# The float64 weights' decode: the sign carried by ScalarE's leaky relu, and the magnitudes written in bfloat16

## The chip, the cores and the metric

The kernel runs on one core of one Trainium2 chip. The metric is device microseconds of that core for one execution. The core has five engines that run their own instruction streams in order and wait for each other by semaphores: TensorE (PE in the profile, its weight loads as PEld), VectorE (DVE), ScalarE (ACT), GpSimd (POOL) and SyncE (SP), which here issues the DMAs.

## The reference

Three blocks follow each other. The inputs are q, k, v of 4 batches, 8 heads, 576 positions, 64 channels.

```
bias   = relu((log1p|i-j| / log1p(max(i,1))) * w1 + b1) @ w2     # per head, 576 x 576
attn   = softmax(q @ k.T / 8 + bias)
x      = attn @ v                                                # 2304 x 512
h      = max(x @ moe_w1, x @ moe_w2, x @ moe_w3)                 # 512 -> 768
x      = h @ moe_w_out                                           # 768 -> 512
h      = x @ moe2_w_in                                           # 512 -> 2048
g      = h where h >= 1, 0 where h <= -1, else (h + 1)^2 / 4
out    = g @ moe2_w_out                                          # 2048 -> 512
```

The six weight matrices of the last two blocks reach the kernel as 64-bit floats: `_layout` hands them over as 64-bit words, and the kernel itself has to turn each into a 32-bit float before it can use it. That turning is the place of the change.

## The kernel before

Every product with a weight is done in three float16 passes: a weight is split into a high float16 part and a low float16 rest (`split`, L155 to L163: ScalarE writes the high part at L158, VectorE the rest at L159), the other operand likewise, and TensorE multiplies high by high, high by low and low by high.

A weight piece is a 128 x 512 block. It goes through these steps:

- `raw_load` (L423): SyncE issues a DMA that brings the block as 64-bit words into a raw buffer.
- `decode` (L430 to L439): four operations on the two 32-bit halves of each word, below.
- `sum_scale` (L448 to L457) or `pair_scale` (L516 to L527): TensorE multiplies the piece's magnitudes with a matrix of ones (L454, L522), so that each column's sum of magnitudes stands in PSUM; VectorE takes the largest (L456, L525) and makes a power of two of it (L137, L138, L142). The magnitudes are read in bfloat16, by `high(y)`.
- `split` by that power of two (L158, L159).

`decode` works on the high word of a 64-bit float (sign, 11 exponent bits, 20 mantissa bits) and on the low word (32 mantissa bits). L435 reads the high word as a 32-bit float and multiplies it by a power of two on ScalarE, which lowers the exponent and keeps the sign; the result is z. L436 makes the top three bits of the low word on ScalarE; that is y. L437 on VectorE shifts z left by three and puts y's bits beside it: y is now the magnitude as a 32-bit float, the shift having pushed the sign out. L438 on VectorE takes the sign bit of z and puts it on y: z is now the weight. `high(y)` is the upper 16 bits of every 32-bit word of y, a bfloat16 with a step of two.

There are 56 pieces. `conv_moe` (18 of them, three per call, names `ws`, `ab`, `aw` for the raw buffers) decodes in place and puts y where the split weight will stand; `conv_wo` (6, raw buffer `ws`); `late_pieces` (32, two at a time), whose raw buffers are `ws` and `v`, whose z is a tile `sp` from a pool of four that the softmax shares, and whose y is the place where the weight will live (`ab`, `masks`, `rw`, `xtab`, `ws`, `k`). The next raw load into a buffer can start only when both L435 and L436 have read it.

Around this, attention runs in 144 slots. A slot's scores come from TensorE (L662), VectorE adds the bias and takes the row's extreme (L674), ScalarE exponentiates (L676), ScalarE and GpSimd split the result in two float16 parts (L692, L693, L694), a DMA transposes them (L696; in half of the first block's slots TensorE transposes instead, L681 to L688), and TensorE multiplies by v (L716). The first MLP (L771 to L783, then L793 to L799) and the bias of the next blocks are mixed in between, then the second MLP follows: L1002 to L1044 for the first block, L1080 to L1131 for the rest. The program fixes each engine's order of instructions when it is built: a scheduler lays the instructions out by priority and by a timeline that it plans, so a change in one helper moves others on every engine.

Of the kernel before, what the change touches and what calls it, by code (L numbers as in the profile page):

```python
# [8 lines left out]
BF16 = mybir.dt.bfloat16  # L9
F32 = mybir.dt.float32  # L10
U32 = mybir.dt.uint32
I64 = mybir.dt.int64
AF = mybir.ActivationFunctionType
ALU = mybir.AluOpType
# [6 lines left out]
def kernel(ctx: ExitStack, tc: tile.TileContext, qt, kt, vr, small, mw1, mw2, mw3, mwo, win, wo2, out):  # L21
# [7 lines left out]
    V, A, G, T, SP = nc.vector, nc.scalar, nc.gpsimd, nc.tensor, nc.sync  # L29
# [135 lines left out]
    if True:  # L165
# [73 lines left out]
        for j in range(5):  # L239
            i0, n = BLK[j][0], BLK[j][1]  # L240
# [16 lines left out]
        for g in range(4):  # L257
            p = slice(32 * g, 32 * g + 32)
# [171 lines left out]
        def decode(r, z, y):  # L430

            w = r.bitcast(U32).rearrange("p (n two) -> p n two", two=2)
            if z is None:
                z = w[:, :, 1]
            A.activation(z.bitcast(F32), w[:, :, 1].bitcast(F32), AF.Copy, scale=2.0 ** -112)  # L435
            A.activation(y, w[:, :, 0], AF.Copy, scale=2.0 ** -29 * (1 - 2.0 ** -20), bias=-0.5)  # L436
            V.scalar_tensor_tensor(y, z, 3, y, ALU.logical_shift_left, ALU.bitwise_or)  # L437
            V.scalar_tensor_tensor(z, z, 0x80000000, y, ALU.bitwise_and, ALU.bitwise_or)  # L438
            return z.bitcast(F32)  # L439

        def high(y):

            return y.bitcast(BF16).rearrange("p (n two) -> p n two", two=2)[:, :, 1]

        def by_k(t):
            return t.rearrange("p (k f) -> p k f", k=KK)
# [1 line left out]
        def sum_scale(s, ys):  # L448

            pn = mlp_ps()  # L450
            for i, y in enumerate(ys):
                yb = high(y)
                for k in range(KK):
                    T.matmul(pn[:, P * i:P * i + P], ones, yb[:, P * k:P * k + P], start=(k == 0), stop=(k == KK - 1))  # L454
            t = st([P, 1], F32, "tcol")
            V.tensor_reduce(t, pn[:, :P * len(ys)], AX.X, ALU.max)  # L456
            pow2_inverse(s, t, 14)  # L457

        def conv_moe(ft):

            zs, ys = [], []
            for i in range(3):
                ys.append(wm[:, ft, i].rearrange("p s k c -> p (s k c)").bitcast(U32))
                zs.append(decode(moe_raw[3 * ft + i], None, ys[-1]))
            s = c_sn[:, ft:ft + 1]
            sum_scale(s, ys)
            for i in range(3):
                split(wm[:, ft, i, 0], wm[:, ft, i, 1], by_k(zs[i]), s, WENG[i])
            if ft == 0:
                moe_load(4)  # L470
            if ft == 3:
                moe_load(5)

        def conv_wo():

            zs = []
            for ft in range(NF1):
                raw_load(mwo[P * ft:P * ft + P, :], raws[:, ft % 2])
                y = rt_[:, ft % 2]
                zs.append(decode(raws[:, ft % 2], zt[:, ft] if ft < 5 else rt_[:, 0], y))  # L480
                sum_scale(c_sm[:, ft:ft + 1], [y])
                yield
            t = newcol(NF1)
            V.tensor_tensor(t, c_sn, c_sm, ALU.mult)
            V.tensor_reduce(c_kap, t, AX.X, ALU.min)
            inv2(t, c_sn)
            V.tensor_scalar(c_sm, t, c_kap, None, ALU.mult)
            for ft in range(NF1):
                split(wo16[:, ft, 0], wo16[:, ft, 1], zs[ft], c_sm[:, ft:ft + 1], "v")
                yield  # L490
# [25 lines left out]
        def pair_scale(s, ys, k):  # L516

            pn = mlp_ps()
            for i, y in enumerate(ys):
                yb = high(y)  # L520
                for kk in range(KK):
                    T.matmul(pn[:, P * i:P * i + P], ones, yb[:, P * kk:P * kk + P], start=(kk == 0), stop=(kk == KK - 1))  # L522
            n = s.shape[1]
            t = st([P, 2], F32, "tcol2")[:, :n]
            V.tensor_reduce(t, pn[:, :2 * P].rearrange("p (n c) -> p n c", n=n), AX.X, ALU.max)  # L525
            floor2(t, t)
            inv2(s, t, k)  # L527

        def late_pieces():
# [19 lines left out]
            for y in range(len(spec) // 2):  # L549
                load(2 * y + 2)  # L550
                dst = [late_home(2 * y + i) for i in range(2)]
                zs = [decode(loaded[2 * y + i], st([P, S], F32, "sp")[:, :512].bitcast(U32), dst[i].bitcast(U32)) for i in range(2)]
                load(2 * y + 3)
                q = y // 2
                s = c_sq2[:, q:q + 1] if y % 2 else c_sp[:, 2 * q:2 * q + 2]
                pair_scale(s, [d.bitcast(U32) for d in dst], 12 if y % 2 else 14)
                for i in range(2):
                    split(dst[i][:, 0:512], dst[i][:, 512:1024], zs[i], s[:, 0:1] if y % 2 else s[:, i:i + 1], PENG[y % 2])
                yield
                yield  # L560
# [580 lines left out]
        for x in range(len(work) + GL):  # L1141
            if x < len(work):
                y, sub, ft = work[x]
# [17 lines left out]
            if x >= GL:  # L1161
                y, sub, ft = work[x - GL]
# [48 lines left out]
```

## Time and profile before

| what | value |
|---|---|
| median of 3 runs | 1063.61 us (1061.68 to 1063.82) |
| span of the profiled execution, first to last instruction | 1056.6 us |
| time around the span: median less span | 7.0 us |
| PE busy | 948.6 us, 90% |
| DVE busy | 753.9 us, 71% |
| ACT busy | 572.4 us, 54% |
| POOL busy | 489.5 us, 46% |
| the chain that ended last, by engine | PE 55%, DVE 19%, DMA 8%, ACT 6%, POOL 5% |

The profile is of one execution that is not among the three timed ones, so its own whole time is known as its span, and the 7.0 us are the difference to the median of the runs. Busy time is an average over stages with different limits; the stages used here are cut by time: 38 to 125 us (the first slots, and all of `conv_moe`), 125 to 240 (`conv_wo`), 240 to 470, 470 to 590, 590 to 690 us (most of `late_pieces`), and from 690 us on, where no weight is decoded.

### The profile page before, as it was taken

The numbers are of one execution on the slowest core, as the hardware profiler recorded it, in microseconds if no ns is written. First come the engines' busy times: TensorE is split into PE (matmuls) and PEld (weight loads), VectorE is DVE, ScalarE is ACT, GpSimd is POOL, SyncE is SP. The second block draws the span as 40 slices with busy tenths as digits, with TensorE's granted clock in tenths as the row PEclk, the third lists the DMA queues.
The fourth block names the chain that finished last, engine by engine and source line by source line (L and its number), as shares of the span: only waits on it lengthen the run. The fifth ranks groups of instructions, "written<-read, shape, count | busy, mean of one in ns | idle before, by whom it ended". The sixth has DMA issues, their size and how long they took to land.

```text
span 1056.6 us, 26035 instructions
## 1 busy us (share of the span) xinstructions
PE 948.6 (90%) x10298; PEld 772.4 (73%) x10298; DVE 753.9 (71%) x1686; ACT 572.4 (54%) x1146; POOL 489.5 (46%) x705
## 2 busy tenths in 40 slices
PE   6787879799999989999899779989999999999993
PEld 5555768687788878777678667634588888888882
DVE  8989977887546677566475498698787586676662
ACT  4487665675665545775666466543344444444441
POOL 1032335577667754655456121887035344444340
PEclk7586789899999989999899899999999999999997
DMA  9796757599999888999997843010020010000000
GB/s 293 209 273 176 207 153 150 146 224 205 229 231 208 183 177 163 216 223 213 205 240 170 176 165 115 21 40 1 1 81 21 1 42 21 1 22 21 1 21 20
DMA packets 229437, 139.10 MB, mean 132 GB/s; under 512 B 177988, under 2 KB 208196, under 8 KB 228804
## 3 DMA queue, kind: packets, MB, share of 16 engines
q1 hardware_dynamic: 229316, 137.45, 54.9%
q8 instruction: 80, 1.31, 0.5%
q14 instruction: 41, 0.34, 0.1%
HBM read 79.68 MB, written 15.27 MB: 90 GB/s over the span
## 4 chain that ended last, share of the span: by engine, by line
PE 55%; DVE 19%; DMA 8%; ACT 6%; POOL 5%; issue 4%; SPq 1%; DVEq 0%; POOLq 0%; ACTq 0%
PE pm L1080 13%; PE pm L771 13%; PE s L1119 11%; PE s L662 6%; PE pav L716 3%; PE pm L793 3%; DVE sp L674 3%; DMA ws<-in_moe_w_out_dram 2%; PE s L1028 2%; PE pm L375 2%; DMA v<-in_moe_w_in_dram 1%; DVE aw L159 1%; DMA xT<-px 1%; ACT sp L676 1%; DVE phl L1020 1%
## 5 line engine op out<-in xcount | busy, mean ns | idle before, releaser
L771 PE MATMUL pm<-xT,aw 128*128 128x256 f16 (+1 forms) x2160 | 243.6, 266 | 17.0 <-DVE pt L688 4.4
L771 PEld LDWEIGHTS <-aw 128*128 128x128 f16 x2160 | 190.8, 100 | 55.2 <-issue 28.2
L676 ACT ACTIVATE sp<-sp,mx 128x576 f32<-128x576 f32 x144 | 110.5, 768 | 91.6 <-DVE mx L674 91.4
L694 POOL TENSOR_TENSOR phl<-sp,phl 128x512 f16<-128x512 f32 x128 | 154.4, 1206 | 0.1
L662 PE MATMUL s<-k,qz 64*128 64x288 f32 (+1 forms) x576 | 138.5, 470 | 12.2 <-DVE mx L674 11.4
L693 POOL TENSOR_TENSOR phl<-sp,phl 128x64 f16<-128x64 f32 x128 | 47.8, 373 | 211.9 <-ACT phl L692 151.8
L1097 ACT ACTIVATE sp<-pm,vec 128x256 f32<-128x256 f32 x112 | 61.3, 556 | 93.9 <-PE pm L1080 93.8
L674 DVE CUSTOM_DVE_ANT_0 sp<-s,ab 128x576 f32<-128x576 f32 x128 | 93.2, 749 | 18.8 <-PE s L662 10.3
L662 PEld LDWEIGHTS s<-k,qz 64*128 64x128 f32 (+1 forms) x576 | 75.7, 205 | 37.4 <-DVE mx L674 15.7
L1080 PEld LDWEIGHTS <-ab 128*128 128x128 f16 x840 | 82.1, 98 | 10.3
L793 PE MATMUL pm<-hh,wo 128*128 128x256 f16 x648 | 79.0, 276 | 11.5 <-ACT hh L782 7.4
L716 PEld LDWEIGHTS <-pt 128*128 128x128 f16 x1792 | 73.9, 99 | 15.6 <-issue 6.2
L692 ACT ACTIVATE phl<-sp 128x576 f16<-128x576 f32 x128 | 84.2, 672 | 1.0
L783 POOL TENSOR_TENSOR hh<-hm,hh 128x256 f16<-128x256 f32 (+1 forms) x60 | 41.7, 696 | 88.6 <-ACT hh L782 87.2
L1101 POOL TENSOR_TENSOR hh<-hh 128x128 f32<-128x128 f32 x56 | 32.7, 584 | 107.5 <-DVE hh L1099 101.2
L1098 DVE SCALAR_TENSOR_TENSOR hh<-pm,vec,sp 128x256 f32<-128x256 f32 x112 | 52.7, 478 | 35.0 <-ACT sp L1097 34.7
L793 PEld LDWEIGHTS <-wo 128*128 128x128 f16 x648 | 62.5, 99 | 20.3 <-issue 11.8
L716 PE MATMUL pav<-v,pt 128*128 128x64 f16 x1568 | 71.0, 195 | 2.6 <-ACT pt L685 1.5
L778 DVE SCALAR_TENSOR_TENSOR hm<-pm,hm 128x256 f32<-128x256 f32 (+1 forms) x120 | 46.9, 391 | 31.6 <-PE pm L771 15.8
L1119 PEld LDWEIGHTS <-xT 128*128 128x128 f16 x588 | 57.4, 98 | 7.8 <-ACT xT L1106 1.2
L1119 PEld LDWEIGHTS <-wo 128*128 128x128 f16 x588 | 57.5, 98 | 6.7
L1102 POOL TENSOR_TENSOR hh<-hh 128x128 f32<-128x128 f32 x56 | 25.8, 460 | 68.8 <-DVE hh L1099 64.1
(281 smaller groups left out, 1979.3 us busy)
## 6 DMA issues: line engine op xcount, KB each, us to landing
k<-in_k_dram SPq DMA_DIRECT2D x64, 288.0 KB, 4.3
v<-v_d SPq DMA_DIRECT2D x24, 640.0 KB, 5.1
ws<-in_moe_w_out_dram SPq DMA_DIRECT2D x15, 512.0 KB, 5.7
ws<-in_moe_w_in_dram SPq DMA_DIRECT2D x11, 512.0 KB, 4.8
x_d<-hl SPq DMA_DIRECT2D x36, 128.0 KB, 2.4
qz<-in_q_dram SPq DMA_DIRECT2D x16, 256.0 KB, 5.1
ab<-in_moe_w_dram SPq DMA_DIRECT2D x8, 512.0 KB, 8.7
qz<-x_d SPq DMA_DIRECT2D x4, 1024.0 KB, 4.8
```

Of the source, the lines that this page charges most:

```text
L662: T.matmul(sbox[i + r][:, c, :288], q[p, s if u.j == SJ else s // 2], k[p, 288 * c:288 * c + 288], start=True, stop=True)
L674: V.tensor_tensor_reduce(halves(sn), sbox.pop(i)[:, :, :288], halves(bias_sb[u.j][:, h]), -0.125, 3e38, ALU.add, ALU.min, mx)
L676: A.activation(pf, sn, AF.Exp, scale=-1.0, bias=mx, accum_out=u.sums[:, h:h + 1])
L692: A.activation(hl[:, :S], pf, AF.Copy)
L694: G.tensor_tensor(hl[:, S + 64:], pf[:, :512], hl[:, :512], ALU.subtract)
L716: T.matmul(u.pav[:, 64 * h:64 * h + 64], pt[:, c], v[:, sl, 64 * (h % 4):64 * (h % 4) + 64], **kw)
L771: T.matmul(o, wm[:, ft, i, wp, kk], x_rhs(key, xp, kk) if n == 256 else x_rhs(key, xp, kk)[:, c], start=(x == 0), stop=(x == 11))
L793: T.matmul(pm, wo16[:, ft, wp, P * d:P * d + P], hh[:, ft, hp], start=(ft == 0 and y == 0), stop=(ft == NF1 - 1 and y == 2))
L1080: T.matmul(pm, w[:, wp, kk], x2t[ORDER[y]][:, kk, xp, 256 * sub:256 * sub + 256], start=(x == 0), stop=(x == 11))
L1097: A.activation(r, pm, AF.Relu, scale=c_ch[:, f], bias=c_half)
L1098: V.scalar_tensor_tensor(t, pm, c_c[:, f], r, ALU.mult, ALU.max)
L1119: T.matmul(m[x], gl[:, gp, i], w[:, wp], start=(start and z == 0 and x % 2 == 0), stop=(stop and z == 2 and (x % 2 == 1 or x == 6)))
```

## The change

In `decode`, L435 turns from a copy with a scale into a leaky relu, in which positive and negative inputs get different powers of two. For a positive high word x the result is x times 2^-112, as before. For a negative one it is |x| times 2^-80: a positive number whose exponent is larger by 32. After the shift by three that difference sits in the sign bit, so that L437 alone yields the signed weight, in z. The second VectorE operation is gone. L438 is now a ScalarE operation that writes the weight's magnitude as bfloat16 into the first half of y's memory, and `high(y)` reads 512 bfloat16 values there, one beside the other. Per piece the kernel has three ScalarE operations and one VectorE operation where it had two and two; line numbers are the same before and after.

```diff
-            A.activation(z.bitcast(F32), w[:, :, 1].bitcast(F32), AF.Copy, scale=2.0 ** -112)
+            A.activation(z.bitcast(F32), w[:, :, 1].bitcast(F32), AF.Prelu, scale=-(2.0 ** -80), alpha=-(2.0 ** -32))
             A.activation(y, w[:, :, 0], AF.Copy, scale=2.0 ** -29 * (1 - 2.0 ** -20), bias=-0.5)
-            V.scalar_tensor_tensor(y, z, 3, y, ALU.logical_shift_left, ALU.bitwise_or)
-            V.scalar_tensor_tensor(z, z, 0x80000000, y, ALU.bitwise_and, ALU.bitwise_or)
+            V.scalar_tensor_tensor(z, z, 3, y, ALU.logical_shift_left, ALU.bitwise_or)
+            A.activation(high(y), z.bitcast(F32), AF.Abs)
             return z.bitcast(F32)
 
         def high(y):
 
-            return y.bitcast(BF16).rearrange("p (n two) -> p n two", two=2)[:, :, 1]
+            return y.bitcast(BF16)[:, 0:512]
```

The order of instructions moves with it. The first place is VectorE at the end of the first bias, where the first six pieces (`ws`, `ab`, `aw`) are put together between the first rows of the softmax (L674, named ISA here). A piece of the difference, - before, + after:

```order
-L437 SCALAR_TENSOR_TENSOR aw<-ws,aw 128x512 x2
-L437 SCALAR_TENSOR_TENSOR aw<-ab,aw 128x512
+L437 SCALAR_TENSOR_TENSOR ws<-ws,aw 128x512 x2
+L437 SCALAR_TENSOR_TENSOR ab<-ab,aw 128x512
 L437 SCALAR_TENSOR_TENSOR aw<-aw 128x512 x3
 L233 TENSOR_SCALAR btmp<-ident,tcol 128x128
 L674 ISA sp,mx<-s,ab 128x576
 L674 ISA mx 128x1
-L438 SCALAR_TENSOR_TENSOR ws<-ws,aw 128x512
 L288 TENSOR_SCALAR xtab<-xtab,vec 128x576
-L438 SCALAR_TENSOR_TENSOR ws<-ws,aw 128x512
-L438 SCALAR_TENSOR_TENSOR ab<-ab,aw 128x512
```

L437 now writes where the high word stood instead of y, and L438 no longer stands between the softmax's rows. The second place is ScalarE at the same time, from the last L435 of the first twelve pieces on:

```order
 L435 ACTIVATE aw<-aw 128x512 x3
 L435 ACTIVATE ab<-ab 128x512 x3
-L676 ACTIVATE sp,sums<-sp,mx 128x576
-L692 ACTIVATE phl<-sp 128x576
-L676 ACTIVATE sp,sums<-sp,mx 128x576 x2
+L438 ACTIVATE aw<-ws 128x512 x2
+L438 ACTIVATE aw<-ab 128x512
+L438 ACTIVATE aw<-aw 128x512 x3
```

All six L438 now stand ahead of the first exponential, L676. The third place is ScalarE in `late_pieces`, around 600 us. Before:

```order
L436 ACTIVATE ab<-v 128x512
L435 ACTIVATE sp<-v 128x512
L436 ACTIVATE ab<-ws 128x512
L776 ACTIVATE hm<-pm 128x256
L435 ACTIVATE sp<-ws 128x512
L782 ACTIVATE hh<-hm 128x256
```

The same place after the change:

```order
L436 ACTIVATE ab<-v 128x512
L438 ACTIVATE ab<-sp 128x512
L435 ACTIVATE sp<-v 128x512
L782 ACTIVATE hh<-hm 128x256
L776 ACTIVATE hm<-pm 128x256
L435 ACTIVATE sp<-ws 128x512
```

L438, which waits for VectorE's L437 of its piece, now stands ahead of an L435, and L436 of the piece in `ws` comes later than it did. SyncE issues the same DMAs, some of them in another order. ScalarE's order holds two table loads, at L219 and L249, before and after.

## Rows read from the trace of the kernel before

**Rows 1.** Busy us per stage: PE, PEld, DVE, ACT, POOL; clock, DMA
```profile
38.00:125.00 87.00, 68.61 (x512) 49.71 (x512) 78.38 (x169) 55.95 (x107) 24.27 (x30) 0.67 0.70 193
125.00:240.00 115.00, 101.44 (x1505) 84.18 (x1504) 94.65 (x225) 74.14 (x172) 63.34 (x82) 0.91 0.79 178
240.00:470.00 230.00, 220.75 (x2982) 186.19 (x2981) 145.50 (x355) 138.97 (x332) 143.86 (x196) 0.99 0.97 202
470.00:590.00 120.00, 104.25 (x1362) 84.67 (x1356) 69.22 (x160) 76.02 (x167) 63.84 (x88) 0.96 0.95 203
590.00:690.00 100.00, 87.81 (x735) 69.55 (x736) 78.06 (x217) 57.96 (x117) 37.29 (x37) 0.98 0.37 115
```

**Rows 2.** The same stages, VectorE's L438 alone: busy us (instructions)
```profile
38.00:125.00 87.00, 14.16 (x18) 0.67 0.70 193
125.00:240.00 115.00, 4.09 (x6) 0.91 0.79 178
240.00:470.00 230.00, 2.58 (x4) 0.99 0.97 202
470.00:590.00 120.00, 9.97 (x11) 0.96 0.95 203
590.00:690.00 100.00, 11.61 (x17) 0.98 0.37 115
690.00:1057.00 367.00, 0.00 (x0) 0.98 0.06 21
```

**Rows 3.** Chain that ended last, 38 to 125 us: start, us, what
```profile
44.08 0.60 DVE ws L438
...
50.45 0.02 ACT sp L676
...
75.83 3.30 ACT aw L436 x6
79.14 0.55 ACT ws L435
...
114.81 0.13 DVE ab L438
```

**Rows 4.** PE's waits, 38 to 125 us: total, times, longest
```profile
PE s L662 <- DVE mx L674: 9.4, 6, 3.1
...
PE pm L235 <- DVE btmp L233: 2.4, 2, 1.7
```

**Rows 5.** Groups of instructions: count, busy us, mean ns, idle before
```profile
L438 DVE SCALAR_TENSOR_TENSOR sp<-sp,ab 128x512 uint32<-128x512 uint32 x18 | 12.9, 729 | 0.0
...
L692 ACT ACTIVATE phl<-sp 128x576 f16<-128x576 f32 x128 | 84.2, 672 | 1.0
...
L435 ACT ACTIVATE sp<-ws 128x512 f32<-128x512 f32 x20 | 12.6, 666 | 0.4 <-DVE ab L159 0.3
...
L1015 ACT ACTIVATE sp<-pm,vec 128x512 f32<-128x512 f32 x16 | 12.2, 768 | 7.2 <-PE pm L1002 7.2
...
L249 ACT ACT_TABLE_LOAD x1 | 1.3, 1283 | 0.0
```

**Rows 6.** ScalarE's first exponential, with its idle time before it
```profile
44.11 0.78 ACT L676 ACTIVATE sp<-sp,mx 128x576 f32<-128x576 f32 x1 [7.20 <-DVE mx L674]
```

**Rows 7.** Chain, 125 to 240 us, by line: shares of 115 us
```profile
by line: PE pm L771 26.4%; PE s L662 15.8%; PE pm L375 8.9%; DMA ws<-in_moe_w_out_dram 7.7%; PE pav L716 7.1%; issue 3.5%; DVE aw L159 2.8%; PE pm L681 2.7%; DVE masks L371 2.7%; DVE sp L674 2.3%; DVE pt L687 2.3%; DVE ws L438 2.1%; PE pm L
```

**Rows 8.** Chain that ended last, 590 to 690 us: start, us, what
```profile
597.66 0.69 ACT sp L435
...
617.00 0.16 DVE sp L438
...
652.61 0.60 DVE sp L438
...
686.73 0.72 ACT phl L1019
```

**Rows 9.** SyncE's waits before its issues, 595 to 660 us
```profile
SPq L423 <- ACT sp L435: 27.7, 7, 7.7
```

## The prediction

> **What bounds the kernel now.** I read the stages first: busy time of each engine in five stretches, with the granted clock [rows 1]. From 240 to 470 us TensorE works 220.75 of 230 us: what leaves VectorE there leaves no time. From 38 to 125 us the picture is another one: VectorE is busy 78.38 of 87 us (90%), TensorE 68.61 at a mean clock of 0.67 of full speed, ScalarE 55.95. VectorE sets this stage. Between them lie 125 to 240 us (TensorE 88%, VectorE 82%), 470 to 590 us (TensorE 87%) and 590 to 690 us (TensorE 88%, VectorE 78%). After 690 us no weight is decoded.
>
> Then I read where the operation that goes, L438, stands: 18 of the 56 in the first of these stages with 14.16 us, 6 in the second with 4.09, 4, 11 and 17 in the others with 2.58, 9.97 and 11.61, none later [rows 2]. All of it is 42.4 us of VectorE's time, and most of that is beside the path. The chain of waits says how much is on it. From 38 to 125 us the chain passes through L438 in 13 pieces, the first at 44.08 us and the last at 114.81 us, together 9.07 us [rows 3]. From 125 to 240 us it holds 2.1% of 115 us, 2.4 us [rows 7]. From 590 to 690 us four pieces lie on it, the first and the last at 617.00 and 652.61 us, together 1.96 us [rows 8]. Last I read TensorE's waits in the first stage: 9.4 us for the extreme of a softmax row (L674, six times) and 2.4 us for a small VectorE result, 11.8 us together [rows 4]. That is the most that a faster VectorE can give back there directly.
>
> **The change part by part.** *The VectorE operation that goes.* A L438 takes 729 ns in its largest group [rows 5], and 0.60 us when the next follows at once [rows 3]. On the chain it is worth 9.1 us in the first stage, 2.4 in the second and 2.0 in the last. The other 15, between 240 and 590 us, lie beside a busy TensorE; I put them at nothing, with under 1 us if that cover were gone in some slots.
>
> *The ScalarE operation that comes.* The trace of before has no absolute value from a 32-bit float to bfloat16. The nearest rows are L692, from float32 to float16 on 576 columns, 672 ns, and L435, 512 columns, 666 ns, which bound it from both sides; a ScalarE operation that follows another at once costs less, six L436 lie on the chain in 3.30 us, 0.55 us each [rows 3, 5]. I take 0.55 us. Its 56 make 31 us of ScalarE's time. How much of that comes on the path I take from ScalarE's present share: in the first stage the chain holds 11 pieces of ScalarE, the first at 50.45 us, the last at 79.14 us, 9.26 us of 55.95 busy, or 17% [rows 1, 3]; 18 x 0.55 x 0.17 = 1.7 us. From 590 to 690 us it holds 29 pieces, the first at 597.66 us, the last at 686.73 us, 17.29 us of 57.96 busy, or 30% [rows 1, 8]; 17 x 0.55 x 0.30 = 2.8 us. The first six are free: they now stand ahead of the first exponential, but ScalarE sat idle 7.20 us before that one [rows 6], longer than the 3.3 us they take. If that cover were gone, they would cost 3.3 us; I leave them in the 18, as the dearer reading.
>
> The Trainium skill, "ScalarE: Activation LUTs", section Rules for kernel authors, speaks against the move: simple pointwise functions belong on VectorE, which it puts at up to about three times ScalarE's rate in bfloat16. In this trace the two engines are level on this piece, 729 ns against 666 ns [rows 5], since the operation that goes has two 32-bit inputs. By the page an operation moved would be dearer by its factor; by the rows it costs what it saves, and the measured rows decide.
>
> *The sums wait longer.* Before, they could begin behind the first VectorE operation; now they need L437, then ScalarE's L438. That is 0.55 us more per piece, but VectorE, which must take the maximum of the sums afterwards, no longer has a second L438 in front of that. 0.60 us less against 0.55 us more: nothing, within half a microsecond a pair.
>
> *Leaky relu for copy.* Both are one pass of ScalarE. Bounds: from 0 (L435's copy, 666 ns) to 0.10 us more (L1015, a relu with per-partition scale and bias out of PSUM, 768 ns) [rows 5]. I take 0; the upper end is 5.6 us of ScalarE in all, some 1.3 us on the path by the shares above.
>
> *Contiguous bfloat16 for the sums.* TensorE's ones products (L454, L522) keep their shapes. Reading every second value may have cost something or nothing; at nothing, since TensorE waits for others where they stand.
>
> **What is late next, and the sum.** In the first stage 9.1 - 1.7 = 7.4 us would go if nothing else were late. But VectorE already idles 8.6 of 87 us there, ScalarE rises to about 66 us, TensorE runs at a low clock, and two of the instructions on ScalarE's new order wait for L437 where VectorE waits for L676's output: a new alternation. I take 80%, 6.0 us. In the second stage TensorE is at 88% and takes over soon: half of 2.4, 1.2 us. In the last: 2.0 off, 2.8 on, 0.8 us lost. The reordering that the change brings elsewhere I put at nothing, with 3 us either way in the range. Sum: 6.0 + 1.2 - 0.8 = 6.4 us. The profiled span of 1056.6 us becomes 1050.2; with the same 7.0 us around it, by which the span stands below the median of the runs of 1063.6, the time is 1057.2 us, 0.6% less.
>
> **The rivals.** *No change: ScalarE takes over in the first stage.* For it: ScalarE runs its instructions in order, exponentials stand behind L438s that wait for VectorE, and ScalarE's share there rises from 64 to 76%. Against it: that share and VectorE's new one, (78.4 - 14.2)/87 = 74%, each leave a quarter of the stage free. Then half of the 7.4 us remain, 3.7, the second stage gives nothing, and the last takes 2.8: 0.9 us less, 1062.7.
>
> *Slower: the loop of raw loads from 590 to 690 us.* A load needs a raw buffer that ScalarE has read: SyncE waited 27.7 us, seven times, for L435 [rows 9]. Now L438s stand ahead of L435s on ScalarE, and each waits for VectorE's L437 first. If all 17 come into that loop, with 0.55 us each and as much as one VectorE operation of 0.68 us of waiting, it grows by 17 x 1.23 = 20.9 us, less the 2.0 us that go, 18.9; part of it has TensorE's 12 us of idle time there to hide in, say 6, so 13 us are lost. With half of the early gain, 3.7, and nothing in the second stage the time is 1073. The point from which it decides is a loss of more than 7.2 us in this stage, 0.42 us a piece. Against it: VectorE loses two operations a pair in the same loop, and L435s moved ahead of an L436 that waited for its load.
>
> *More: VectorE's time goes whole.* All of the chain's L438 goes, 9.1 + 2.4 + 2.0 = 13.5 us, and ScalarE's new ones stay in its idle time: 1050.1. For it: ScalarE is idle 31 us of the first stage and 42 of the last [rows 1]. Against it: engines that wait for each other in order seldom give back all.
>
> *The function needs another table.* ScalarE would load its table for the leaky relu and again for the exponential. On its new order decodes and exponentials change places 32 times; at 1283 ns a load [rows 5] that is 41 us: 1098. Against it: the built order shows two table loads, as before. The Trainium skill, "ScalarE: Activation LUTs", section Table sets: the hidden batching unit, names relu, copy, identity and abs as found in every set, and not the leaky relu; the two loads of the order speak for one set.
>
> **How the numbers follow.** The forecast has 50 in 100, no change 18, slower 15, more 16, the table 1. The range that holds 8 in 10 reaches from 1050.0, the case of more, to 1068.0, into the slower one; the likeliest case's own is 1053 to 1061, by the bounds of the leaky relu and the reordering. A difference under 0.2%, 2.1 us, can't be told from none here: faster means under 1061.5, which holds the forecast but for a hundredth, the case of more and a quarter of no change, 69 in 100; 14 are within, 17 above 1065.7.
>
> **What would show it.** In the changed profile: VectorE's busy time down by about 40 us to 714, ScalarE's up by about 31 to 603, with two table loads. The first MLP's first product (L771) some 6 us earlier, and a smaller sum of waits for L674. The stretch from there to 590 us as long as before. L438 on ScalarE near 0.6 us, in the chain rarely. The stage of the late pieces, from the last attention slot to the first product of L1002, longer by less than 2 us. The forecast is wrong if the first MLP starts at the same time, if SyncE's waits for L435 grow by more than 7 us, or if stretches without a decode change their length by more than 3 us.

## The result and the profile after

The changed kernel takes 1051.01 us, median of 5 runs (1048.15 to 1057.18), against 1063.61 us (1059.34 to 1065.28) for the kernel before in the same session: a ratio of 0.990, 95% interval 0.988 to 0.992. A second session gave 1053.56 against 1061.76 us, 0.9917 (0.9893 to 0.9940). The first trace of after has a span of 1046.3 us in a run of 1048.15, so 1.9 us lie around this span, not the 7.0 us that the prediction put there; in the timed runs of before beside the experiments it is 1.8 to 3.1 us.

Two traces of the changed kernel exist, one of each session; both are compared with the trace of before, in us between the same events:

| stretch | forecast | before | after, first trace | after, second trace |
|---|---|---|---|---|
| 38 us to the first product of L771 | -6.0 | 81.6 | 75.5 (-6.1) | 79.1 (-2.5) |
| from there to the first L793 | -1.2 | 115.3 | 115.3 (0.0) | 113.5 (-1.8) |
| from there to the last exponential | 0 | 342.5 | 341.5 (-1.0) | 343.0 (+0.5) |
| from there to the first L1002 | +0.8 | 96.0 | 92.9 (-3.1) | 94.1 (-1.9) |
| span | -6.4 | 1056.6 | 1046.3 (-10.3) | 1050.9 (-5.7) |

The two traces of one program are 4.6 us apart, most of it in the first stretch; what that is comes below. First the stages of the first trace, columns as in [rows 1]:

```profile
38.00:125.00 87.00, 67.34 (x600) 49.81 (x600) 71.02 (x165) 72.57 (x140) 22.52 (x32) 0.78 0.80 220
125.00:240.00 115.00, 104.01 (x1514) 86.43 (x1513) 87.95 (x216) 75.32 (x176) 65.59 (x88) 0.91 0.75 169
240.00:470.00 230.00, 218.72 (x2945) 183.95 (x2942) 143.04 (x348) 141.61 (x336) 142.80 (x196) 0.99 0.98 203
470.00:590.00 120.00, 108.25 (x1355) 87.81 (x1353) 58.40 (x150) 80.90 (x177) 58.46 (x81) 0.94 0.98 209
590.00:690.00 100.00, 88.64 (x716) 66.66 (x714) 74.57 (x211) 68.77 (x137) 43.05 (x42) 1.00 0.28 94
```

In the first stage VectorE falls from 78.38 to 71.02 us and ScalarE rises from 55.95 to 72.57. TensorE is busy as long as before (67.34 and 68.61 us), but it gets 600 products done instead of 512, at a granted clock of 0.78 instead of 0.67. Over the whole run VectorE falls from 753.9 to 713.7 us and ScalarE rises from 572.4 to 600.9.

Three of the groups of the new L438 on ScalarE, then the pieces of it on the chain from 38 to 125 us, both of after:

```profile
L438 ACT ACTIVATE ab<-sp 128x512 bf16<-128x512 f32 x18 | 11.1, 624 | 0.7 <-DVE sp L437 0.7
...
L438 ACT ACTIVATE aw<-ab 128x512 bf16<-128x512 f32 x8 | 5.5, 684 | 0.0
...
L438 ACT ACTIVATE aw<-aw 128x512 bf16<-128x512 f32 x6 | 4.0, 697 | 0.0
```

```profile
109.13 0.57 ACT aw L438
...
111.20 0.65 ACT aw L438
...
114.70 0.67 ACT aw L438
```

One costs 624 to 697 ns in these groups, where the forecast had 0.55 us; three pieces of the 18 lie on the chain, together 1.89 us (forecast 1.7), where 13 pieces of VectorE's L438 held 9.07 [rows 3]. The leaky relu takes 667 ns in its largest group, as the copy did (666 ns, [rows 5]). Now TensorE's longest waits from 38 to 125 us, to be held against [rows 4]:

```profile
PE pm L318 <- DMA ws<-in_v_dram: 5.5, 2, 2.9
PE s L662 <- DVE mx L674: 4.8, 2, 3.0
PE pm L235 <- DVE btmp L233: 2.7, 1, 2.7
PE s L662 <- issue: 2.1, 2, 1.1
```

The wait for the softmax's extreme (L674) fell from 9.4 to 4.8 us, as forecast. But a new one of 5.5 us stands above it: TensorE waits for V's load, the DMA that brings a batch of v into `ws`. The same wait in before, then in the second trace of after:

```profile
PE pm L318 <- DMA ws<-in_v_dram: 0.8, 1, 0.8
```

```profile
PE pm L318 <- DMA ws<-in_v_dram: 10.4, 3, 5.4
```

In the new order the third group of L318, the products that find V's extreme, stands behind the products of queries and keys of 16 slots; before, it stood behind those of 26. By these sums, what the softmax gave back went into that load. That the wait is nearly twice as long in the second trace is a part of what sets the two apart.

### The profile page after: what moved, and what is told of

It reads as the page before. It is cut to its first block, busy times and chain, and to the rows that moved or that the text cites. A ratio compares the mean times of both kernels' runs of the same rounds, so it can differ in the third digit from the quotient of the medians.

```text
span 1046.3 us, 26045 instructions
## 1 busy us (share of the span) xinstructions
PE 943.4 (90%) x10298; PEld 768.3 (73%) x10298; DVE 713.7 (68%) x1630; ACT 600.9 (57%) x1202; POOL 479.4 (46%) x705
## 4 chain that ended last, share of the span: by engine, by line
PE 55%; DVE 14%; DMA 11%; ACT 8%; POOL 5%; issue 4%; SPq 1%; DVEq 0%; POOLq 0%; ACTq 0%
PE pm L1080 13%; PE pm L771 12%; PE s L1119 11%; PE s L662 7%; PE pav L716 3%; PE pm L793 3%; DMA ws<-in_moe_w_in_dram 2%; PE s L1028 2%; PE pm L375 2%; DVE sp L674 2%; ACT sp L676 2%; DMA pt<-phl 1%; DMA aw<-in_moe_w_dram 1%; DVE phl L1020 1%; PE pm L1002 1%
## 5 line engine op out<-in xcount | busy, mean ns | idle before, releaser
L771 PE MATMUL pm<-xT,aw 128*128 128x256 f16 (+1 forms) x2160 | 241.2, 265 | 13.2 <-ACT hm L776 6.1
L771 PEld LDWEIGHTS <-aw 128*128 128x128 f16 x2160 | 188.8, 99 | 51.6 <-issue 29.4
L694 POOL TENSOR_TENSOR phl<-sp,phl 128x512 f16<-128x512 f32 x128 | 151.6, 1184 | 0.0
L676 ACT ACTIVATE sp<-sp,mx 128x576 f32<-128x576 f32 x144 | 110.7, 769 | 67.2 <-DVE mx L674 67.0
L693 POOL TENSOR_TENSOR phl<-sp,phl 128x64 f16<-128x64 f32 x128 | 44.0, 344 | 221.8 <-ACT phl L692 152.7
L662 PE MATMUL s<-k,qz 64*128 64x288 f32 (+1 forms) x576 | 134.4, 460 | 9.3 <-DVE mx L674 5.9
L674 DVE CUSTOM_DVE_ANT_0 sp<-s,ab 128x576 f32<-128x576 f32 x128 | 93.2, 752 | 27.4 <-PE s L662 13.0
L662 PEld LDWEIGHTS s<-k,qz 64*128 64x128 f32 (+1 forms) x576 | 73.4, 200 | 30.8 <-DVE mx L674 8.0
L793 PE MATMUL pm<-hh,wo 128*128 128x256 f16 x648 | 79.3, 277 | 10.0 <-ACT hh L782 6.7
L716 PEld LDWEIGHTS <-pt 128*128 128x128 f16 x1792 | 74.9, 101 | 15.1 <-issue 6.8
L1101 POOL TENSOR_TENSOR hh<-hh 128x128 f32<-128x128 f32 x56 | 30.1, 538 | 106.9 <-DVE hh L1099 96.1
L793 PEld LDWEIGHTS <-wo 128*128 128x128 f16 x648 | 62.4, 99 | 19.1 <-issue 10.4
L1102 POOL TENSOR_TENSOR hh<-hh 128x128 f32<-128x128 f32 x56 | 25.7, 459 | 72.3 <-DVE hh L1099 67.5
```

Of the source, the lines that this page charges most:

```text
L662: T.matmul(sbox[i + r][:, c, :288], q[p, s if u.j == SJ else s // 2], k[p, 288 * c:288 * c + 288], start=True, stop=True)
L674: V.tensor_tensor_reduce(halves(sn), sbox.pop(i)[:, :, :288], halves(bias_sb[u.j][:, h]), -0.125, 3e38, ALU.add, ALU.min, mx)
L676: A.activation(pf, sn, AF.Exp, scale=-1.0, bias=mx, accum_out=u.sums[:, h:h + 1])
L694: G.tensor_tensor(hl[:, S + 64:], pf[:, :512], hl[:, :512], ALU.subtract)
L716: T.matmul(u.pav[:, 64 * h:64 * h + 64], pt[:, c], v[:, sl, 64 * (h % 4):64 * (h % 4) + 64], **kw)
L771: T.matmul(o, wm[:, ft, i, wp, kk], x_rhs(key, xp, kk) if n == 256 else x_rhs(key, xp, kk)[:, c], start=(x == 0), stop=(x == 11))
```

## The experiments

The names of the theories are those of the expectations. For the first four: V, the time taken off VectorE makes the gain; O, in the late pieces the order on ScalarE makes a third of it by itself; R, the new order of the whole program makes it.

**Which pieces make the gain.** Five kernels use both forms of the decode, chosen by a flag (the flag is handed to `high` as well):

```diff
-        def decode(r, z, y):
+        def decode(r, z, y, old=False):
...
+            if old:
+                A.activation(z.bitcast(F32), w[:, :, 1].bitcast(F32), AF.Copy, scale=2.0 ** -112)
+                A.activation(y, w[:, :, 0], AF.Copy, scale=2.0 ** -29 * (1 - 2.0 ** -20), bias=-0.5)
+                V.scalar_tensor_tensor(y, z, 3, y, ALU.logical_shift_left, ALU.bitwise_or)
+                V.scalar_tensor_tensor(z, z, 0x80000000, y, ALU.bitwise_and, ALU.bitwise_or)
+                return z.bitcast(F32)
```

New decode for the 18 early pieces alone:

> New decode in conv_moe alone (18 pieces, all before 125 us); the 6 pieces of conv_wo and the 32 late ones as before. Theory V (VectorE's time in the first stage): first MLP product (L771) near 113.5 us as with the whole change (119.6 before), last softmax exponential about 6 us earlier, nothing more gained behind it: the first L1002 near 667 us, 6 us of time gone, ratio about 0.994. Rival O (the order on ScalarE in the late pieces gave a third of it by itself): the same here. Rival R (the builder's new order as a whole, not the operation, made the gain): the first MLP product not earlier than 117 us.

New decode for the 32 late pieces alone:

> New decode in the 32 late pieces alone. All theories: first MLP product at 119.6 us as before. V and O: from the last softmax exponential to the first L1002 3 us shorter than before (93 us instead of 96), time 2 to 4 us under before, ratio about 0.997. R: that stretch differs by less than 1 us or is longer.

The early pieces alone gave 0.9996 (0.9969 to 1.0023), where V and O had 0.994; the late alone gave 0.9974 (0.9953 to 0.9994), as V and O had it. That doesn't add up to 0.990, although the trace of the early ones shows the first product of L771 at 113.0 us, 6.6 us earlier than before. This trace is of a run of 1054.42 us; the median of the twelve is 1061.28, and no run near it was traced. So three more combinations were run.

Early and late:

> The new decode for the 18 early pieces and the 32 late ones; the 6 pieces of the MLP's output weights keep the old one, with its second VectorE operation. A (the parts add up): 1.000 for the early by 0.997 for the late, 0.997, about 1058 us, and the six pieces are worth the other 0.7% of the whole. V: the six pieces stand where TensorE is busy from 125 us on and hold 4 us of VectorE at most, so nearly all of the gain is here, 0.990 to 0.993, about 1052. C (clock): as V, with 8 us or more between runs by their mean clock.

The six pieces of the MLP's output weights alone:

> The new decode for the 6 pieces of the MLP's output weights alone; the 18 early and the 32 late pieces keep the old one. A (each part has its own worth, and the whole is their product): the whole at 0.991 over 0.999 for early and late together leaves 0.992 for these six, about 1053 us. V (VectorE's time): six pieces are 4 us of VectorE beside a TensorE that is busy 88% of 125 to 240 us, 0.998 to 1.001, about 1061. I (the parts need each other: the early gain is lost again, in most runs, behind a stage in which the old decode of these six is late): 0.998 to 1.001 here, and the gain appears only in the next kernel.

Early and these six:

> The new decode for the 18 early and the 6 pieces of the MLP's output weights, the 32 late pieces old. A and I both expect the whole's 0.991 without the late part's 0.997: 0.993 to 0.995, about 1056 us; V expects the early part's 1.000 by at most 0.2% for the six: 0.997 to 1.000, about 1060. In the profile the stretch from the first MLP product to the first L793 is as long as before or up to 2 us shorter, where the early part alone made it 2.3 us longer; from the last exponential to the first L1002 it is within 1 us of before, since the late pieces are the old ones.

| new decode for | ratio, 95% interval | runs, us |
|---|---|---|
| 18 early | 0.9996 (0.9969 to 1.0023) | 1053.5 to 1068.7 |
| 32 late | 0.9974 (0.9953 to 0.9994) | 1054.8 to 1065.8 |
| six | 1.0027 (1.0009 to 1.0045) | 1059.8 to 1067.7 |
| early and late | 0.9992 (0.9967 to 1.0016), without the longest run | 1053.1 to 1070.6 |
| early and six | 0.9939 (0.9917 to 0.9962) | 1051.0 to 1056.2 |
| all | 0.990 (0.988 to 0.992), 0.9917 (0.9893 to 0.9940) | 1048.2 to 1057.2 |

A, in which each part has a worth of its own, falls; I, in which the parts need each other, stands: early and six alone give 1.000 and 1.003, and together 0.994. With the late pieces' 0.997 that makes 0.991, the whole. V, which prices each part by VectorE's time alone, misses here as well: it had 0.990 to 0.993 for early and late and 0.997 to 1.000 for early and six. With the early pieces new and the six old, the runs of one program spread over 15 us and more. The second trace of the kernel with early and late was taken for this:

> The kernel with the new decode for the early and the late pieces once more, for a second trace: its runs lay between 1053 and 1070.6 us, and the one trace of it is of the fastest. I1: in a slow run the first stage itself falls back: granted clock from 38 to 125 us 0.67 to 0.72, first MLP product at 117 to 122 us, against 0.80 and 112.1 in the fast one; the later stages are as in the fast one. I2: the first stage keeps its clock of 0.78 or more and its product at 112 to 115 us, and the time goes between there and the first L793, where the old decode of the six pieces stands: that stretch, 122.8 us in the fast one, is over 126. If the run is again one at 1053 to 1056 us, it tells the two apart only in so far as the first stage repeats.

That run took 1059.89 us, the first traced one 1053.09. (The expectation's 122.8 us was miscounted: from L771 to L793 the first trace has 118.7 us, the second 120.3.) The first stage repeats (clock 0.78, first product at 114.5 us), so I1 falls; but I2's place is only one of several. The second trace falls behind in steps: 1.8 us up to the exponential at 112 us, 3.1 us from 131 to 143 us (in the 10 us behind it the clock is 0.67, in the first trace 1.00), and 2.9 us from 268 to 280 us. For the last, TensorE in the first trace, then in the second (start, us, what, idle time before it and its releaser):

```profile
273.93 0.27 PE L801 MATMUL pm<-hh,wo 128*128 128x256 f16 x1 [1.15 <-ACT hh L790]
...
275.01 2.13 PE L801 MATMUL pm<-hh,wo 128*128 128x256 f16 x18
...
278.65 4.10 PE L801 MATMUL pm<-hh,wo 128*128 128x256 f16 x36
```

```profile
279.61 0.30 PE L801 MATMUL pm<-hh,wo 128*128 128x256 f16 x1 [2.77 <-ACT hh L790]
...
280.96 3.19 PE L801 MATMUL pm<-hh,wo 128*128 128x256 f16 x18
...
285.66 4.11 PE L801 MATMUL pm<-hh,wo 128*128 128x256 f16 x36
```

(L801 here is L793 of the other listings, shifted by 8 lines.) One wait is 2.77 us instead of 1.15. Behind the longer one the next 18 products take 3.19 us instead of 2.13, since the clock fell from 2.4 to 1.2 GHz for a part of them (the granted clock from 280 to 290 us is 0.84, in the first trace 1.00); the 36 after that are level again. The wait itself costs 1.6 us, the clock 1.1 more.

At 210 us there is another wait of this kind. The kernels with early pieces new and the six old (three traces) wait there for VectorE's L382, a bias; neither of the two traces of after nor the one of early and six does, nor does before. (The kernel with two extra VectorE operations, below, waits there for 1.08 us though its six pieces are new; that points to VectorE's time as what brings the wait.) The first trace of early and late:

```profile
208.36 1.23 PE L670 MATMUL s<-k,qz 64*128 64x288 f32 x4
210.90 0.64 PE L375 MATMUL pm<-coef,masks 128*128 128x64 f16 x16 [1.30 <-DVE ab L382]
211.56 2.28 PE L670 MATMUL s<-k,qz 64*128 64x288 f32 x4
```

Its second trace:

```profile
212.25 1.23 PE L670 MATMUL s<-k,qz 64*128 64x288 f32 x4
215.33 1.04 PE L375 MATMUL pm<-coef,masks 128*128 128x64 f16 x16 [1.85 <-DVE ab L382]
216.29 2.28 PE L670 MATMUL s<-k,qz 64*128 64x288 f32 x4
```

And after, at the same place (L662 is that L670):

```profile
208.96 1.48 PE L771 MATMUL pm<-xT,aw 128*128 128x256 f16 x12
...
210.62 0.63 PE L375 MATMUL pm<-coef,masks 128*128 128x64 f16 x16
...
211.24 1.23 PE L662 MATMUL s<-k,qz 64*128 64x288 f32 x4
```

Four products that take 1.23 us take 2.28 behind a wait of 1.3 or 1.85 us. In the trace of the early pieces alone the wait is there too (1.91 us), and the clock did not fall behind it: the length of a wait doesn't decide this, and what does was not found. From the first L771 to the first L793 the three traces with the six old and the early new need 117.6, 118.7 and 120.3 us, those with both new 115.3, 113.5 and 115.6. The Trainium skill, "TensorE: Matmul & The Clock Gate", Part 1: The HAM clock gate, warns that the number of products at the low clock when a kernel starts differs between runs of one program, and puts that loss under 1% of a typical span. The falls here lie in the middle of the kernel, of which that passage doesn't speak; two traces of one program differ in them as well, and are 7 us apart, 0.7% of 1058, by them and the waits ahead of them.

**Is it VectorE's time?** The whole change, and two VectorE operations on 224 columns each into a scratch tile behind every decode:

```diff
             A.activation(high(y), z.bitcast(F32), AF.Abs)
+            for o in (0, 224):
+                V.scalar_tensor_tensor(st([P, 224], U32, "scr"), z[:, o:o + 224], 0x80000000, z[:, o:o + 224], ALU.bitwise_and, ALU.bitwise_or)
```

> The whole change, and per piece two more VectorE operations on 224 columns each into a scratch tile that nobody reads, some 0.66 us together, as much as the operation that went. The results are unchanged. V: the gain of the first stage goes, first MLP product at 119 us or later, and the late stretch is as long as before: time 1060 to 1066. O: the first stage loses its gain, the late stretch keeps its 3 us: 1058 to 1061. R or any gain that isn't VectorE's time (contiguous sums, the shape of the dependences): most of it stays, under 1056.

And the change with the magnitude written by VectorE:

```diff
-            A.activation(high(y), z.bitcast(F32), AF.Abs)
+            V.scalar_tensor_tensor(high(y), z.bitcast(F32), -1.0, z.bitcast(F32), ALU.mult, ALU.max)
```

> The whole change, but the magnitude in bfloat16 is written by VectorE (the larger of z and -z) and not by ScalarE: two operations on VectorE, two on ScalarE, as before the change, with the new form of the merge. V: no gain in the first stage, first MLP product 118 to 121 us; time 1059 to 1066, late stretch as before. O: also the late stretch as before, since ScalarE's order is the old one. If ScalarE's absolute value were a cost on the path, this would be under 1051.

Ratios 1.0021 (1.0002 to 1.0040) and 1.0029 (1.0009 to 1.0048), first MLP product at 118.2 and 119.1 us. VectorE is busy 752.9 and 752.8 us over the span, as long as before (753.9): with its time put back the gain is gone, though the first of the two keeps ScalarE's new operation. V is borne out for the whole. Contiguous magnitudes and the new merge, which both kernels keep, don't make the gain. The new order alone (R) isn't tested apart, since the scheduler lays out each of these kernels anew; the comparison of eleven traces below speaks against it. The Trainium skill, "ScalarE: Activation LUTs", section Rules for kernel authors, would have had this maximum on VectorE; here that took the 1.0029 of before where ScalarE's absolute value takes 0.990 to 0.992.

**TensorE's busy time or its waits?** Busy time from 38 us to the first L771 (columns as in [rows 1]), of before, of after's two traces, and of the kernel with the two extra VectorE operations:

```profile
38.00:119.60 81.60, 63.21 (x437) 44.33 (x436) 73.01 (x157) 54.46 (x103) 21.84 (x27) 0.67 0.74 202
```

```profile
38.00:113.50 75.50, 57.17 (x438) 40.81 (x438) 61.81 (x144) 62.87 (x119) 20.18 (x27) 0.75 0.81 219
```

```profile
38.00:117.10 79.10, 58.93 (x437) 41.62 (x435) 62.88 (x147) 64.25 (x120) 20.36 (x27) 0.72 0.76 207
```

```profile
38.00:118.10 80.10, 61.51 (x433) 43.91 (x431) 71.29 (x168) 61.02 (x115) 21.13 (x27) 0.66 0.78 202
```

Subtract TensorE's column from the length: TensorE idles 18.4, 18.3, 20.2 and 18.6 us. In all eleven traces with nearly the same products (433 to 438) it is 18.3 to 20.8. The 6.1 us of the first trace are 6.0 us of busy time: the same products at a higher clock, 5.3 us of it in the 92 products of queries and keys (35.76 us before, 30.47 after). The second trace is 3.6 us longer than the first, half of it idle and half of it busy time. The clock parts the eleven by VectorE's work on the early pieces. In the six traces in which VectorE is busy 61.6 to 64.6 us (four programs) the granted clock of this stretch is 0.72 to 0.77, and the first L771 comes at 112.1 to 117.1 us; in the five others, in which VectorE is busy 71.3 to 75.1 us (five programs, the two with VectorE's time put back among them), it is 0.66 to 0.68, at 118.2 to 122.8 us. So less work on VectorE there goes with a higher clock in each of the eleven. Why nearly the same idle time leaves a higher clock is not shown.

The next two kernels tried to set the clock by itself: eight products of ones by ones behind the products of queries and keys of each pair of slots up to slot 23, 88 in all, into a part of the scores' tile that nobody reads.

```diff
                     T.matmul(sbox[i + r][:, c, :288], q[p, s if u.j == SJ else s // 2], k[p, 288 * c:288 * c + 288], start=True, stop=True)
+            if 1 <= i < 24:
+                for x in range(8):
+                    T.matmul(sbox[i][:, x % 2, 384:512], ones, ones, start=True, stop=True)
```

With the whole change, which was also timed again beside it:

> The whole change again, in more runs and beside the three kernels of this group. V (VectorE's time in the stages sets the gain): ratio 0.988 to 0.992, about 1051 us, as before. A (the parts add up): the early pieces alone gave 1.000 and the late alone 0.997, so the whole should be near 0.997, 1058 us, and the first result of 0.990 would be five lucky runs. C (the gain comes through TensorE's granted clock): the runs spread over 8 us or more, the time falling as the mean granted clock of the run rises, and the median lies between, 1051 to 1056; the first MLP product starts at 114 us in a run with a mean clock near 0.947 and near 119 in one at 0.937.

> The whole change, and behind each product of queries and keys of slots 1 to 23 eight small products of ones by ones (bfloat16, 128 columns) into a part of the scores' tile that nobody reads: work for TensorE in the time in which it waits for the softmax. It leaves nothing out. C (clock): the granted clock from 38 to 125 us rises from 0.78 to 0.85 or more, the first MLP product comes 1 to 4 us earlier than the changed kernel's 113.5, ratio 0.985 to 0.989. V (VectorE's time): the clock may rise, but the first MLP product stays at 113 to 115, or comes up to 3 us later by the time that the fillers take, ratio 0.990 to 0.993.

With the decode of before:

> The kernel before with the same fillers on TensorE, decode unchanged. C (clock): with the granted clock from 38 to 125 us raised from 0.67 to 0.80, the first MLP product comes at 114 to 116 us where it came at 119.6, without any change of VectorE's work: ratio 0.994 to 0.996, about 1055. V (VectorE's time): VectorE is busy 78 of these 87 us all the same, the product stays at 119 to 122 and the ratio at 0.999 to 1.003.

The whole again gave 0.9917, which V and C both allow and A does not. In its six runs the time falls as the mean clock rises, from 1056.3 us at 0.937 to 1051.6 at 0.950, as C has it; but they spread over 4.7 us, not 8, and the traced one, at 0.949, has its first product at 117.1 us, where C had 114.

The fillers did not do what was wanted. On after the ratio is 0.9996 (0.9979 to 1.0014; one run of 2410.6 us is left out), on before 1.0126 (1.0093 to 1.0160). The clock from 38 to 125 us is 0.67 on after, where it was 0.78 without them, and 0.70 on before, where it was 0.67. The first L771 comes at 120.9 and 128.9 us. C and V both miss, and the pair is inconclusive: the clock couldn't be raised apart from the rest. Up to the first L771 of after with the fillers, all work, then the fillers alone (PE and PEld):

```profile
38.00:120.80 82.80, 73.98 (x517) 51.64 (x516) 66.84 (x149) 66.97 (x125) 19.58 (x29) 0.66 0.78 202
```

```profile
38.00:120.80 82.80, 8.50 (x81) 6.19 (x81) 0.66 0.78 202
```

VectorE has 66.8 us of work there, against 73.0 before, but TensorE's own takes 65.5 us (73.98 less 8.50), and there is no gain. That fits the clock as the path by which the gain comes; it doesn't prove it, since the fillers take 8.5 us of TensorE in the same stretch. On before the order changed too, and TensorE waits up to the first L771 for V's load, where it waited 0.8 us without the fillers:

```profile
PE pm L318 <- DMA ws<-in_v_dram: 11.6, 4, 5.9
```

The last one puts L318 later, since after waits there for V's load:

```diff
-        vm=[0, 0, 6, 11],
+        vm=[0, 0, 8, 14],
```

> The whole change with the products that find V's extreme (L318) two and three slots later (slots 8 and 14 for 6 and 11); all is computed. In the changed kernel they stand after the 16th and the 38th product of queries and keys, where the kernel before had them after the 26th and the 40th, and TensorE waits there 5.5 us for V's load from 38 to 113 us. D (that wait holds the stage): the wait falls below 2 us, the first MLP product comes 2 to 4 us earlier than at 113.5 to 117, ratio 0.986 to 0.989, about 1049. T (TensorE's time at its granted clock holds it, and idle time moves to another wait): the idle time to the first MLP product stays at 18 to 20 us, ratio 0.990 to 0.994, about 1053, by the clock of the run.

The ratio is 0.9962 (0.9938 to 0.9985), worse than the change itself. The wait for V's load did not go away, it moved (TensorE, start and us):

```profile
109.50 1.89 PE L318 MATMUL pm<-ws 128*128 128x128 bf16 x16 [2.33 <-DMA ws<-in_v_dram]
...
118.16 0.58 PE L318 MATMUL pm<-ws 128*128 128x128 bf16 x4 [4.71 <-DMA ws<-in_v_dram]
```

Up to 113 us it is 2.3 us, where D had less than 2; with the second one it is 7.0 us, more than the 5.5 of after. So D is not tested by this kernel. Its order also puts some of the first MLP's products ahead, the first at 98.4 us, so that this event can't be held against the others; the first L793 comes at 232.1 us, where the two traces of after have it at 228.8 and 230.6. T's ratio is missed as well, and its idle time can't be read here. No kernel tried here beats the change.

**The late stage.** From the last exponential to the first L1002 the eight traces in which ScalarE writes the late pieces' magnitude need 92.4 to 94.1 us, mean 93.4; the six in which it doesn't need 95.3 to 97.6, mean 96.2. That stretch in before, in after, and in the kernel with the two extra VectorE operations:

```profile
577.40:673.40 96.00, 77.85 (x821) 67.69 (x818) 72.55 (x218) 53.58 (x114) 23.58 (x26) 0.96 0.51 140
```

```profile
570.30:663.20 92.90, 77.78 (x821) 67.62 (x819) 60.35 (x198) 63.50 (x135) 23.04 (x26) 0.96 0.50 144
```

```profile
584.80:677.30 92.50, 79.07 (x821) 68.66 (x820) 71.94 (x238) 63.83 (x134) 23.76 (x26) 0.94 0.49 145
```

In the third, VectorE is as busy as before (71.94 and 72.55 us), and the stretch is short all the same. So here the gain isn't VectorE's time, and V misses; O, which had this stretch short, is borne out so far. Here it is TensorE's idle time that moves: 18.2, 15.1 and 13.4 us in these three, 12.3 to 15.1 in the eight traces, 15.6 to 18.2 in the six. What moves with it is SyncE's wait for L435 before a load, 27.7 us before [rows 9]; here in the same stretch of after, and in the kernel whose magnitude is written by VectorE:

```profile
SPq L423 <- ACT sp L435: 15.5, 6, 6.0
```

```profile
SPq L423 <- ACT sp L435: 27.0, 8, 7.4
```

It is 15.5 to 21.8 us in the eight, 27.0 to 28.6 in the six. That the shorter wait makes the gain is therefore likely, but it was not changed by itself, and which exchange on ScalarE frees the raw buffer sooner was not isolated.

## Why the prediction was right, and where not

*The whole* was forecast at 1057.2 us, 6.4 us less than before; measured were 12.6 us less in the first session and 8.2 in the second. The way and the range of 1050.0 to 1068.0 are right; the first median, 1051.0, lies outside the likeliest case's own 1053 to 1061. Between the traces the span falls by 10.3 and 5.7 us. In the second that is near the forecast's 6.4 by luck: its terms are -2.5, -1.8, +0.5 and -1.9 us, not -6.0, -1.2, 0 and +0.8.

*The first stage* came out as forecast in the first trace (-6.0, measured -6.1) and at less than half in the second (-2.5). The step that carried it, L438 off the chain and a smaller sum of waits for L674, happened. The step behind it, that this shortens TensorE's waits, failed: V's load took the place, TensorE's idle time stayed at 18 to 20 us, and the gain is the higher clock of the same products. Nor is a smaller sum of waits for L674 enough: with the two extra VectorE operations it is 4.6 us up to the first product of L771, and that product comes at 118.2 us. The prediction read the mean clock of 0.67 in [rows 1] and gave it no term. The right size was partly luck; between the two traces this term moves with the clock and with the wait for V's load.

*From 125 to 240 us* the forecast was half of the chain's 2.4 us of L438. Measured 0.0 and -1.8. But the six pieces do more than that: without them the median of the runs is that of before, whatever the early pieces gain in the trace. A price for each group of pieces can't show that; the sum treated the stages as independent.

*The stage of the late pieces* is the term that failed: +0.8 forecast, -3.1 and -1.9 measured. It counted 2.8 us of ScalarE on the chain by ScalarE's earlier share, and missed that SyncE waits less for L435 in the new order. [Rows 9] showed the wait; the prediction used it for the rival of the slower loop alone. That rival put 18.9 us more into it; the wait fell by 12.2 and 11.4 us in the two traces instead.

*240 to 590 us and after 690 us* were put at nothing: measured between the first L793 and the last exponential -1.0 and +0.5, and at most 0.1 behind the first L1002.

*The 7.0 us around the span* were wrong: an execution and its span are about 1.9 us apart, so the profiled run of before would have a time of some 1058.5 us, 5 us under the median. So the traces of after, 2.9 and 0.8 us under the medians of their runs, are compared with one of before that is 5 us under its own. The forecast span of 1050.2 lies between the two measured ones, 1046.3 and 1050.9; with 1.9 us around it the forecast would have been 1052.1, against medians of 1051.0 and 1053.6.

*The rivals.* ScalarE did not take over the first stage: it is busy 72.57 of 87 us, more than the 66 forecast and about as long as VectorE, and three of its L438 are on the chain. "More" had the right size (1050.1) for the wrong reason: it wanted all of the chain's L438 back, 13.5 us. No further table loads came.

## What to carry to other kernels

Where TensorE waits in pieces of one to three microseconds, the granted clock is a term of its own: split a stage into TensorE's busy and idle time before and after, and see which of the two moved. Parts of a change that remove waits may be worth nothing alone and a good deal together (here 1.000, 1.003 and 0.994). One wait that is left can cost the clock what the other part had won: that is seen at single places here, not shown for the whole difference. A loop of loads that waits for a reader may gain from a new order on the reader's engine, even where that engine has got more work.

## What the runs showed of the hardware

TensorE's clock was found lower behind waits as short as 1.3 us: of the five named here, those of 1.30, 1.85 and 2.77 us were followed by products at 1.2 GHz (four L662 in 2.28 us instead of 1.23, 18 L793 in 3.19 instead of 2.13), those of 1.15 and 1.91 us were not. In part by this the same program has traces 7 us apart. In the timed runs of early and late together the time tends to fall as the run's mean granted clock rises, from 1070.6 us at 0.929 to 1053.1 at 0.945, with exceptions (1061.9 at 0.944, 1058.4 at 0.949). Small products put behind the products of queries and keys did not raise the clock of the changed kernel (0.67 with them, 0.78 without) and raised that of the kernel before a little (0.70 and 0.67); both took longer.
